# First K and Q chunks: two heads in 128 partitions and whole 128x112 TensorE transposes, with the order of all engines written anew

## The chip, the cores and the metric

The kernel runs on one core of one Trainium2 chip. The metric is device time in microseconds (us), from the first to the last instruction and what lies around them. Matrix products run on TensorE (PE; PEld is its weight load), elementwise work on VectorE (DVE), ScalarE (ACT) and GpSimd (POOL), and SyncE (SP) issues most of the DMAs.

## The reference

A recurrent attention (delta rule) over 4 batches x 8 heads, 768 steps, head size 48, and a feed-forward layer on its result:

```python
k_n = k / (np.linalg.norm(k, axis=-1, keepdims=True) + 1e-06)
for t in range(S):                       # per batch and head, state is 48x48
    y[t] = q[t] @ state
    v_old = state.T @ k_n[t]
    state = state + beta[t] * outer(k_n[t], v[t] - v_old)
x = y as [3072 tokens, 384]
h = x @ w_in                             # [3072, 2048], weights are float64
g = h * tanh(log(1 + exp(h)))            # mish
out = (g @ w_out).astype(float32)        # [3072, 384]
```

The weights reach the chip as float64 bit patterns (12.6 MB in all) and are turned on it into a high and a low single-precision part.

## The kernel before, in words

**Tiling.** The 768 steps are cut into 12 chunks of 64 steps. The 32 (batch, head) pairs stand as 16 pairs of heads; one head of a pair uses partitions 0 to 63, the other 64 to 127, and `h` 0 or 1 names the first or second 8 pairs. For a chunk the kernel forms `kt`, the keys with head size in partitions (48 rows at 0 or at 64), the products `pg` of keys with keys, a triangular solve of them on DVE in small column steps (`early`, tiles `pr` and `gt`), merges on PE (`ma`, `mb`), then the products `ta`, `tb`, `gq`, `pz`, and at the end `py`, `ps` (output and new state of the chunk). The first two chunks are solved together by `early(0)`.

**Feed-forward.** The chunk's output is transposed (`xt`) and goes through `g1` (tile `h`, 18 products of 128x256 for each of 8 pieces of the layer) and `g2` (tile `acc`, 12 products of 128x384 each), on all 12 chunks. PE does this in the gaps of the attention of later chunks.

**Weights.** There are 28 weight tiles, `ri` (512 KB each, of `w_in`) and `ro` (384 KB each, of `w_out`). `convert` clamps the upper words on DVE (L1328), scales them on ACT (L1331), shifts and joins the words on DVE (L1341, L1345), rounds on ACT (L1349) and forms the low part on PE, ACT or by an adding DMA (L1357, L1361, L1366, L1368). The first `mish` on ACT waits until 21 tiles have passed L1331.

**Start.** `loads` issues the DMAs in the order of the list `d0` (here `"k0","k1","b","a","q",2,"v",...`, a number being so many weight tiles). The keys of chunk 0 are loaded straight into `xx`, where the state update of the chunk wants them (`load_k`), those of chunk 1 and the queries of chunk 0 into plain tiles `kn1`, `qn0` (`load_plain`), each with 64 partitions for one head of the pair. `turn_k` and `turn_q0` turn them with `turned`, one product with a 64x64 identity for each head: 16 for each half of a chunk. Ahead of a key turn a product with zeros (L1405) fills the whole PSUM tile, since the turned rows leave gaps. `keep_warm` puts products with zeros (`warm`, L1868, 107 in all) on PE where it would stand still.

**What sets the order.** Every engine's order is fixed by the program. The table `TT` gives each step a rank, and the program is issued in that rank; an engine does its own instructions in that order and waits where one is not ready. `SLOT` gives each tile a buffer. The program gives its DMAs eight counters in turn: a DMA is issued once the one that had its counter before it has landed.

Of the kernel before, what the change touches and what calls it, by code (L numbers as in the profile page):

```python
# [10 lines left out]
F32 = mybir.dt.float32  # L11
# [9 lines left out]
F64_MOST = 122879.9921875  # L21
LOW = 'pppppppppddddddddddddddddddd'
# [7 lines left out]
def bcast_in(ap, n):  # L30
# [5 lines left out]
    'loadk0': [0],  # L36
    'warm0.501': [1],
    'warm30.601': [2],
    'loadk1': [3],
    'loadi1': [4],  # L40
    'turn_k(0,0)': [5],
    'loadq': [6],
    'turn_k(0,1)': [7],
    'loado13': [8],
    'turn_k(0,0).0>1': [9],
    'early0': [10, 20, 23, 24, 31, 41, 43, 48, 52, 54, 55, 56, 57, 61, 62, 64, 67, 74, 77, 79, 85, 86, 93, 104, 106, 107, 111, 113, 117, 121, 122, 131, 140, 141, 142, 507, 922],
    'turn_k(1,0)': [11],
    'loada': [12],
    'loadb': [13],
    'unit(1,)': [14],  # L50
    'early0.0>1': [15],
    'turn_k(0,1).0>1': [16],
    'turn_k(1,0).0>1': [17],
    'turn_k(1,1)': [18],
    'loadi0': [19],
    'turn_k(1,1).0>1': [21],
    'early0.1>1': [22],
    'loado2': [25],
    'loadi2': [26],
    'early0.2>1': [27],  # L60
    'warm46.601': [28],
    'warm11.802': [29],
    'early0.3>1': [30],
    'warm12.1': [32],
    'loado1': [33],
    'cv1': [34, 63, 73, 76, 95, 139, 145, 177, 1062],
    'turn_beta()': [35],
    'turn_q0(0,)': [36],
    'cv0': [37, 45, 58, 70, 78, 144, 149, 173, 728],
# [12 lines left out]
    'loadi3': [60],
    'warm11.503': [65],
    'cv25': [66, 123, 200, 289, 509, 510, 514, 520, 529],
    'warm11.502': [68],
    'cv5': [69, 112, 164, 189, 190, 198, 201, 230, 1378],
    'warm12.2': [71],
    'loadi4': [72],
    'warm11.9': [75],
    'warm29.5': [81],  # L90
    'warm0.601': [82],
    'loado0': [83],
    'cv11': [84, 96, 234, 249, 264, 275, 281, 308, 478],
# [2022 lines left out]
```

## Time and profile before

| | us |
|---|---|
| median of 3 runs | 654.91 (654.89 to 658.72) |
| the profiled execution | 655.69 |
| its span, first to last instruction | 653.8 |
| PE busy | 629.3 (96%) |
| DVE busy | 383.2 (59%) |
| ACT busy | 288.4 (44%) |
| POOL busy | 78.5 (12%) |

The busy shares are means over stages with different limits, so the profile is read by stage: the lead (up to about 83 us, where the first chunk's `py` starts), the stretch in which the feed-forward starts while weights are still converted (to about 165 us), and the rest. A row of the trace gives the start and length in us, the engine, the line, the output and input tiles, the number of instructions merged, and in brackets the idle time before and what ended it. The profile counts a single-precision product with an identity of 64 as two instructions.

### The profile page before, as it was taken

The page shows a single profiled execution, that of the slowest core. Times are in us where ns is not written, and L with a number is a line of the kernel's source. Part 1 is how long each engine was busy: PE and PEld are TensorE (multiplying, and loading weights), DVE is VectorE, ACT ScalarE, POOL GpSimd, SP SyncE. Part 2 cuts the span into 40 slices and gives each one's busy share as a digit, 9 for nine tenths or more (in the row PEclk, how much of TensorE's full clock was granted, in tenths as well). Part 3 has the DMA queues.
Part 4 walks back from the last instruction along what each step waited for, and adds up shares of the span by engine and source line. Part 5 has one row for each costly group of instructions (what it writes and reads, how often), then busy time and mean ns, then how long its engine had stood idle before and what let it go on. Part 6 is the DMA issues. An engine that isn't in the chain of part 4 may idle for free.

```text
span 653.8 us, 22428 instructions
## 1 busy us (share of the span) xinstructions
PE 629.3 (96%) x9881; PEld 584.3 (89%) x9890; DVE 383.2 (59%) x834; ACT 288.4 (44%) x556; POOL 78.5 (12%) x117
## 2 busy tenths in 40 slices
PE   8899899998999999999999999999999999999997
PEld 6664679998989988999899999999989999999996
DVE  1376679999597998674866737667543322412120
ACT  2233688844464344433542445433434534333241
POOL 5011022234100130020200010210011100000000
PEclk9999799999999999999999999999999999999999
DMA  9996056963312333223123231312301312001011
GB/s 237 322 266 119 4 89 99 164 110 74 58 23 45 70 50 50 53 34 58 36 45 55 46 55 26 57 20 38 61 2 32 70 27 49 2 2 25 1 24 25
DMA packets 155600, 42.84 MB, mean 66 GB/s; under 512 B 146384, under 2 KB 150992, under 8 KB 155504
## 3 DMA queue, kind: packets, MB, share of 16 engines
q1 hardware_dynamic: 150608, 36.73, 28.0%
q0 software_dynamic: 2736, 4.20, 3.8%
q8 instruction: 78, 1.28, 0.8%
q10 hardware_dynamic: 2160, 0.49, 0.4%
q14 instruction: 18, 0.15, 0.1%
HBM read 32.47 MB, written 4.72 MB: 57 GB/s over the span
## 4 chain that ended last, share of the span: by engine, by line
PE 70%; DVE 12%; SPq 6%; DMA 4%; ACT 3%; issue 3%; POOL 0%; DVEq 0%; POOLq 0%
PE acc L1843 23%; PE h L1809 22%; SPq L1271 6%; PE gq L1650 4%; PE warm L1868 3%; PE py L1650 3%; PE pg L1464 2%; PE kp L1398 2%; PE pz L1650 2%; DVE g L1826 2%; DVE pr L1522 2%; PE ps L1650 2%; DVE gt L1524 2%; PE tb L1650 1%; PE ta L1650 1%
## 5 line engine op out<-in xcount | busy, mean ns | idle before, releaser
L1809 PE MATMUL h<-x,wi 128*128 128x256 f32 x1728 | 221.8, 284 | 2.6 <-ACT e L1824 2.6
L1843 PE MATMUL acc<-wo,g 128*128 128x384 f32 x1152 | 218.7, 341 | 0.1
L1809 PEld LDWEIGHTS h<-x,wi 128*128 128x128 f32 x1728 | 212.9, 188 | 6.6 <-ACT e L1824 3.2
L1843 PEld LDWEIGHTS acc<-wo,g 128*128 128x128 f32 x1152 | 198.9, 188 | 2.0 <-DVE g L1826 0.5
L1826 DVE TENSOR_TENSOR g<-e,g 128x512 fp32r<-128x512 f32 x96 | 67.1, 703 | 118.6 <-ACT g L1825 118.3
L1824 ACT ACTIVATE e<-h 128x512 f32<-128x512 f32 x96 | 57.3, 598 | 79.8 <-PE h L1809 61.6
L1825 ACT CAST g<-e 128x512 fp32r<-128x512 f32 x96 | 59.0, 620 | 71.3 <-PE acc L1843 70.5
L1522 DVE TENSOR_TENSOR pr<-gt 128x58 f32<-128x58 f32 (+9 forms) x164 | 60.3, 368 | 3.9
L1524 DVE TENSOR_TENSOR gt<-gt,pr 128x58 f32<-128x58 f32 (+9 forms) x164 | 58.1, 355 | 3.9
L1628 POOL TENSOR_TENSOR vt<-vt,ne 128x384 f32<-128x384 f32 x24 | 22.3, 941 | 203.4 <-DMA vt<-in_v_dram 123.6
L1635 DVE STREAM_TRANSPOSE xx<-xx 128x1024 f32<-128x1024 f32 x20 | 24.8, 1241 | 32.1 <-DMA xx<-in_q_dram 27.8
L1650 PE MATMUL gq<-xx,kt 48*64 48x112 f32 (+1 forms) x768 | 42.1, 256 | 1.2 <-issue 1.0
L1707 DVE TENSOR_TENSOR xx<-gq,amask 64x256 f32<-64x256 f32 x96 | 40.2, 419 | 4.8 <-PE gq L1650 4.1
L1650 PEld LDWEIGHTS py<-xx 128*64 128x64 f32 x768 | 37.8, 138 | 4.1 <-issue 1.8
L1650 PE MATMUL py<-xx 128*64 128x48 f32 x768 | 41.2, 224 | 0.1
L1650 PEld LDWEIGHTS pz<-vt,tt 64*64 64x64 f32 x768 | 33.8, 138 | 7.3 <-issue 4.4
L1650 PEld LDWEIGHTS gq<-xx,kt 48*64 48x64 f32 x768 | 37.0, 133 | 2.4 <-issue 2.2
L1650 PE MATMUL pz<-vt,tt 64*64 64x48 f32 x768 | 37.5, 234 | 1.2 <-issue 1.2
L1650 PE MATMUL ps<-xx 128*48 128x48 f32 x704 | 37.6, 208 | 0.0
L1729 ACT COPY xx<-pz 64x384 f32<-64x384 f32 x48 | 22.8, 475 | 26.4 <-PE gq L1650 20.1
L1704 DVE TENSOR_TENSOR vt<-vt,gq 128x192 f32<-128x192 f32 x44 | 15.4, 351 | 32.2 <-PE gq L1650 31.6
L1557 POOL COPY tt<-d 32x512 f32<-32x512 f32 x40 | 27.6, 690 | 39.7 <-PE pz L1650 21.0
(128 smaller groups left out, 612.3 us busy)
## 6 DMA issues: line engine op xcount, KB each, us to landing
ri<-in_moe_w_in_dram SPq DMA_DIRECT2D x12, 512.0 KB, 7.5
ro<-in_moe_w_out_dram SPq DMA_DIRECT2D x16, 384.0 KB, 7.2
kt<-in_k_dram SPq DMA_DIRECT2D x76, 64.0 KB, 2.9
vt<-in_v_dram SPq DMA_DIRECT2D x48, 96.0 KB, 3.1
out_dram<-o SPq DMA_DIRECT2D x48, 96.0 KB, 2.2
xx<-in_k_dram SPq DMA_DIRECT2D x46, 96.0 KB, 2.9
xx<-in_q_dram SPq DMA_DIRECT2D x80, 32.0 KB, 2.3
wo<-mo POOLq DMA_DIRECT2D x9, 192.0 KB, 3.5
```

The source lines that it names most:

```text
L1271: m = (nc.scalar if turns[0] else nc.sync).dma_start(out=dst, in_=src)
L1522: nc.vector.tensor_tensor(out=pv, in0=nj, in1=xj, op=ALU.mult)
L1524: nc.vector.tensor_tensor(out=below, in0=below, in1=pv, op=ALU.add)
L1557: nc.gpsimd.tensor_copy(out=tt2[r, t2, :, c0:c0 + 32], in_=dts[g][r, t2])
L1635: nc.vector.transpose(x, x)
L1650: last[:] = [nc.tensor.matmul(*a, start=True, stop=True)]
L1707: nc.vector.tensor_tensor(out=x[r, p4, hh, D:D + C], in0=ps[r, :, d:], in1=bcast_mid(amask[r], 4), op=ALU.mult)
L1809: nc.tensor.matmul(h[:, f2, :], wt["i", f * P // WI * NCH + c][:, i2, f0:f0 + P], x[:, c, :], start=(i == 0), stop=(i == 3 * NCH - 1))
L1824: for d, f in ((0.7, lambda: nc.scalar.activation(e, h, AF.Mish)), (0.7, lambda: nc.scalar.copy(out=gg[:, 0], in_=e)), (0.8, lambda: nc.ve ...
L1825: (0.7, lambda: nc.scalar.copy(out=gg[:, 0], in_=e)),
L1826: (0.8, lambda: nc.vector.tensor_tensor(out=gg[:, 1], in0=e, in1=gg[:, 0], op=ALU.subtract))):
L1843: nc.tensor.matmul(acc[t], gg[:, a, f2, ts_], wt["o", f][:, i2, :], start=(f == 0 and i == 0), stop=(f == NF - 1 and i == 2))
```

## The change: what it does

`load_plain` now loads the keys of chunks 0 and 1 and the queries of chunk 0 into a tile of 128 partitions x 8 x 112: partitions 0 to 63 hold 64 steps of one pair of heads, 64 to 127 those of the next pair, and the 112 columns hold both heads of the pair, 48 columns each, with a gap of 16 that DVE sets to zero. `turned` is four TensorE transposes of 128x112 for each half of a chunk, where there were 16 products; the product with zeros is gone. Since the keys of chunk 0 no longer come through `xx`, a new step `"x"` of `d0` loads them there later, from the same place in memory. The copies out of PSUM take 112 partitions instead of 128. `ON_POOL = (0, 0)` leaves both shifts and clamps of `convert` on DVE. The tables `TT` and `SLOT` are written anew, so every engine's order differs in places.

```diff
+ON_POOL = (0, 0)
...
 TT = {
-    'loadk0': [0],
-    'warm0.501': [1],
-    'warm30.601': [2],
-    'loadk1': [3],
+    'warm0.501': [0],
+    'loadk0': [1],
+    'warm11.601': [2],
+    'loadi0': [3],
...
-              dw=51.0, nw=0, d0=["k0","k1","b","a","q",2,"v",3,4,"s",3,"p",5,"k2",4,7,"k3"], un=(21.0, 21.1), tb=8.8,
+              dw=51.0, nw=0, d0=["k0","k1","b","a","q",2,"v",3,"x",4,"s",3,"p",5,"k2",4,7,"k3"], un=(21.0, 21.1), tb=8.8,
...
+    WN = D + C
 
     def load_plain(key, src, both=False):
-        t = nat[key] = placed(mp, "g", 3, [P, NP, D], F32, key)
-        for hh in range(2):
-            turns[0] = both and hh == 1
-            load(t[64 * hh:64 * hh + 64], src[hh])
+        pool, tag, nb = (ap, "kt", 4) if key == "qn0" else (mp, "g", 3)
+        t = nat[key] = placed(pool, tag, nb, [P, PB, WN], F32, key)
+        nc.vector.memset(t[:, :, D:C], 0.0)
+        for pp in range(2):
+            turns[0] = both and pp == 1
+            for hh in range(2):
+                c0 = C - C * hh
+                load(t[C * pp:C * pp + C, :, c0:c0 + D], src[hh].rearrange("t (a b) d -> b t a d", b=2)[pp])
         turns[0] = False
 
-    def turned(ps, h, hh, src):
-        r, r0 = slice(64 * hh, 64 * hh + 64), 64 - 64 * hh
-        for p in range(PB):
-            nc.tensor.matmul(ps[r0:r0 + D, p, :], src[r, p], ident[r, r], start=True, stop=True)
+    def turned(ps, h, src):
+        for a in range(4):
+            nc.tensor.transpose(ps[:WN, 2 * a:2 * a + 2, :].rearrange("p a b -> p (a b)"), src[:, 4 * h + a], ident)
 
     def turn_k(n, h):
...
-        nc.tensor.matmul(ps.rearrange("p a b -> p (a b)"), zb[:, 0:P], zb[:, :512], start=True, stop=True)
-        for hh in range(2):
-            turned(ps, h, hh, nat["kn1"][:, PB * h:PB * h + PB] if n else xx[h][:, :, hh, D + C:])
+        turned(ps, h, nat[f"kn{n}"])
 
         def out():
-            nc.scalar.copy(out=kts[n][:, PB * h:PB * h + PB].rearrange("p a b c -> p a (b c)"), in_=ps)
+            nc.scalar.copy(out=kts[n][:WN, PB * h:PB * h + PB].rearrange("p a b c -> p a (b c)"), in_=ps[:WN])
...
     def turn_q0(h):
...
-        for hh in range(2):
-            turned(ps, h, hh, nat["qn0"][:, PB * h:PB * h + PB])
+        turned(ps, h, nat["qn0"])
...
+        elif x == "x":
+            for h in range(2):
+                load_k(0, h)
+            give("x0")
...
-            if m == 0:
-                for h in range(2):
-                    load_k(0, h, both=True)
-                give("x0")
-            elif m == 1:
-                load_plain("kn1", kk[:, C:2 * C], both=True)
+            if m < 2:
+                load_plain(f"kn{m}", kk[:, C * m:C * m + C], both=True)
```

**PE, the first instructions after the opening `warm` products.** `kp` is the PSUM tile of a turn, `kn` a plain tile of keys. Before:

```order
L1405 MATMUL kp_0_125<-zero 128x512
L1398 MATMUL kp_0_125<-ident,xx_100 48x64 x16
...
L1405 MATMUL kp_1_146<-zero 128x512
L1398 MATMUL kp_1_146<-ident,xx_101 48x64 x16
L1464 MATMUL pg_0_169<-kt_124 32x64 x32
...
L1405 MATMUL kp_0_203<-zero 128x512
L1398 MATMUL kp_0_203<-ident,kn_119 48x64 x16
```

Now:

```order
L1403 MATMUL kp_0_136<-ident,kn_113 112x128 x4
L1403 MATMUL kp_1_141<-ident,kn_113 112x128 x4
L1869 LDWEIGHTS zero
L1869 MATMUL warm<-zero 128x512
...
L1466 MATMUL pg_0_154<-kt_135 32x64 x32
L1466 MATMUL pg_1_191<-kt_135 32x64 x32
L1403 MATMUL kp_0_231<-ident,kn_125 112x128 x4
```

Each turn is four instructions instead of 17, and both halves of chunk 0 have their `pg` before chunk 1 is turned. Before the first turn there are eight `warm` products now, and there were four.

**DVE, from the start to the first transpose of the solve.** `d` takes the masked `pg`; `ri` are weight tiles. Before:

```order
L1254 COPY xx_101<-ident 64x8x48 x2
L1468 TENSOR_TENSOR d_167<-pg_0_169,lmask 128x256
L1468 TENSOR_TENSOR d_167<-pg_1_250,lmask 128x256
L1468 TENSOR_TENSOR d_167<-pg_0_287,lmask 128x256
L1468 TENSOR_TENSOR d_167<-pg_1_320,lmask 128x256
L1476 STREAM_TRANSPOSE gt_364<-d_167 128x1024
```

Now:

```order
L1329 TENSOR_SCALAR ri_121<-ri_121 128x512
L1393 MEMSET kn_125 128x8x16
L1393 MEMSET qn_224 128x8x16
L1342 TENSOR_SCALAR ri_121<-ri_121 128x512
L1346 SCALAR_TENSOR_TENSOR mi_243<-ri_121 128x512
L1329 TENSOR_SCALAR ri_146<-ri_146 128x512
L1470 TENSOR_TENSOR d_152<-pg_0_154,lmask 128x256
L1470 TENSOR_TENSOR d_152<-pg_0_249,lmask 128x256
L1470 TENSOR_TENSOR d_152<-pg_1_191,lmask 128x256
L1329 TENSOR_SCALAR ri_187<-ri_187 128x512
L1470 TENSOR_TENSOR d_152<-pg_1_286,lmask 128x256
L1478 STREAM_TRANSPOSE gt_340<-d_152 128x1024
```

Three clamps of weight tiles stand ahead of the last `d`, and the one of `ri_121` stands ahead of the memset of `kn_125`, the tile that the keys of chunk 1 are turned from.

**SP, where the weights' loads end.** `kt` is the load of chunk 2's keys here, `q` that of chunk 1's queries, `xx_100` and `xx_101` those of keys for the state update. Before:

```order
L1271 DMA ri_918<-in_moe_w_in_dram 128x1024
L1271 DMA ro_938<-in_moe_w_out_dram 128x768
L1271 DMA q_991<-in_q_dram 32x16x32 x8
L1271 DMA ri_1124<-in_moe_w_in_dram 128x1024
L1271 DMA ro_1127<-in_moe_w_out_dram 128x768
L1271 DMA kt_1143<-in_k_dram 32x16x32 x8
L1271 DMA xx_100<-in_k_dram 64x8x48 x2
L1271 DMA xx_101<-in_k_dram 64x8x48 x2
```

Now:

```order
L1272 DMA ro_946<-in_moe_w_out_dram 128x768
L1272 DMA xx_100<-in_k_dram 64x8x48 x2
L1272 DMA xx_101<-in_k_dram 64x8x48 x2
L1272 DMA q_1020<-in_q_dram 32x16x32 x8
L1272 DMA ro_1037<-in_moe_w_out_dram 128x768
L1272 DMA ro_1041<-in_moe_w_out_dram 128x768
L1272 DMA ro_1044<-in_moe_w_out_dram 128x768
L1272 DMA xx_100<-in_k_dram 64x8x48 x2
L1272 DMA kt_1202<-in_k_dram 32x16x32 x8
```

The first two `xx` rows are the new step `"x"`. The load of chunk 2's keys, which stood ahead of the `xx` load of chunk 1 (which waits for `ps` of chunk 0), now stands behind it.

## Rows read from the trace of the kernel before

**Rows 1.** The page's part 4, the chain that ended last, by engine and line.

```profile
PE 70%; DVE 12%; SPq 6%; DMA 4%; ACT 3%; issue 3%; POOL 0%; DVEq 0%; POOLq 0%
```

**Rows 2.** Stages: length, busy us (instructions) of each engine, PE clock, DMA share, GB/s.

```profile
28.00:54.00 26.00, 25.50 (x183) 14.73 (x185) 21.54 (x61) 8.22 (x18) 2.06 (x3) 1.00 0.91 257
54.00:83.00 29.00, 25.09 (x711) 16.80 (x713) 17.36 (x44) 16.33 (x37) 3.14 (x4) 0.88 0.23 51
83.00:165.00 82.00, 78.41 (x1480) 72.88 (x1484) 75.47 (x169) 59.96 (x117) 25.70 (x32) 1.00 0.63 107
165.00:654.00 489.00, 476.55 (x7122) 459.83 (x7120) 265.66 (x556) 198.01 (x376) 39.26 (x57) 1.00 0.22 38
```

**Rows 3.** PE in order of time: start, length in us, line, tiles, count, idle before.

```profile
1.54 1.89 PE L1868 MATMUL warm<-zero 128*128 128x512 bf16 x4 [1.54 <-DVE zero L1224]
...
4.23 3.22 PE L1398 MATMUL kp<-ident,xx 64*48 64x64 f32 x32 [0.38 <-DMA xx<-in_k_dram]
7.39 0.61 PE L1405 MATMUL kp<-zero 128*128 128x512 bf16 x1
...
11.11 1.93 PE L1464 MATMUL pg<-kt 48*32 48x64 f32 x64
...
26.24 1.43 PE L1464 MATMUL pg<-kt 48*32 48x64 f32 x42 [1.55 <-issue]
...
29.85 1.52 PE L1906 MATMUL beta<-spare,eye 16*32 16x192 f32 x16
31.30 5.88 PE L1398 MATMUL qp<-ident,qn 64*48 64x64 f32 x64
37.52 8.21 PE L1868 MATMUL warm<-zero 128*128 128x512 bf16 x34 [0.33 <-issue]
```

**Rows 4.** PE, the transposes that the kernel already does, same columns.

```profile
88.31 0.82 PE L1781 MATMUL xt<-ident,yy 128*128 128x128 f32 x6
```

**Rows 5.** DVE in order of time, the first solve and chunk 2's keys, same columns.

```profile
27.71 0.42 DVE L1468 TENSOR_TENSOR d<-pg,lmask 128x256 f32<-128x256 f32 x1 [3.16 <-PE pg L1464]
28.16 1.92 DVE L1476 STREAM_TRANSPOSE gt<-d 128x1024 f32<-128x1024 f32 x1
...
46.92 0.86 DVE L1707 TENSOR_TENSOR xx<-gq,amask 64x256 f32<-64x256 f32 x2 [3.29 <-PE gq L1650]
...
52.18 1.91 DVE L1534 STREAM_TRANSPOSE tt<-gt 128x1024 f32<-128x1024 f32 x1
...
99.30 1.24 DVE L1433 STREAM_TRANSPOSE kt<-kt 128x1024 f32<-128x1024 f32 x1
```

**Rows 6.** ACT in order of time: the first copy of turned keys, same columns.

```profile
7.49 0.59 ACT L1410 COPY kt<-kp 128x512 f32<-128x512 f32 x1 [3.27 <-PE kp L1398]
```

**Rows 7.** SP's queue in order of time, issue of DMAs, same columns.

```profile
0.82 1.67 SPq L1271 DMA_DIRECT2D xx<-in_k_dram  x2
...
42.30 9.99 SPq L1271 DMA_DIRECT2D q<-in_q_dram  x8
...
53.34 7.31 SPq L1271 DMA_DIRECT2D kt<-in_k_dram  x8
84.81 3.72 SPq L1271 DMA_DIRECT2D xx<-in_k_dram  x4
88.62 5.15 SPq L1271 DMA_DIRECT2D kt<-in_k_dram  x8
```

**Rows 8.** DMA issues from 0 to 60 us: count, KB each, median us to landing.

```profile
ri<-in_moe_w_in_dram SPq DMA_DIRECT2D x12, 512.0 KB, 7.5
...
xx<-in_k_dram SPq DMA_DIRECT2D x2, 96.0 KB, 3.7
```

**Rows 9.** Stretches of 1 us with the granted clock, columns as in rows 2.

```profile
71.00:72.00 1.00, 0.00 (x0) 0.00 (x0) 0.95 (x3) 0.95 (x3) 0.00 (x0) 1.00 0.00 0
...
74.00:75.00 1.00, 1.00 (x34) 0.94 (x32) 0.41 (x2) 0.27 (x1) 0.00 (x0) 0.50 0.00 0
```

**Rows 10.** The chain of waits where chunk 0's output starts: start, length, what.

```profile
82.98 0.25 PE py L1650 x4
```

More of the change, by code (lines that the diff above doesn't have):

```diff
@@ L51 @@
[L51 to L69, printed above, removed]
@@ new lines @@
+    'g2.0.2': [465],
+    'turn(1,).0>1': [466],
+    'g1.0.4.0>1': [467],
+    'g1.0.4.0>2': [471],
+    'g1.0.5.0>1': [473],
+    'g1.0.4.0>3': [474],
+    'turn(1,).0>2': [490],
+    'g1.0.5.0>2': [492],
+    'g1.0.5.0>3': [495],
+    'prep(2,)': [508],
+    'g2.0.3': [511],
+    'turn(1,).0>3': [513],
+    'g2.0.4': [515],
+    'turn(1,).0>4': [516],
+    'g2.0.5': [527],
+    'g1.0.6': [528],
+    'g1.0.6.0>1': [533],
+    'g1.0.6.0>2': [536],
+    'g1.0.6.0>3': [538],
+    'g1.0.7': [539],
@@ new lines @@
+    'g1.3.7': [912],
+    'g1.3.7.0>1': [913],
+    'g1.3.6': [915],
+    'early4.2>1': [916],
+    'g2.3.1': [919],
+    'turn(4,)': [920],
+    'g1.3.5.0>2': [922],
+    'turn(4,).0>3': [924],
+    'g1.3.4': [927],
+    'scale_v(5,1)': [928],
+    'ats_z[4,1]+s_gq[5,0].0>3': [929],
+    'g2.3.2': [930],
+    'turn_q(5,1)': [932],
+    'g1.3.5.0>3': [934],
+    'early4.3>1': [935],
+    'g1.3.4.0>1': [936],
+    'ats_b[5]+s_a[6]': [937],
+    'turn(4,).0>1': [938],
+    'ats_b[5]+s_a[6].0>1': [939],
@@ new lines @@
+    'g1.3.4.0>2': [940],
+    'g2.3.3': [942],
+    'turn(4,).0>2': [943],
+    'g1.3.4.0>3': [944],
+    'turn(4,).0>4': [945],
+    'ats_b[5]+s_a[6].0>2': [946],
+    'ats_z[5,0]+s_gq[5,1]': [947],
+    'g1.4.1': [948],
+    'prep(6,)': [949],
+    'g2.3.4': [950],
+    'g1.3.7.0>2': [951],
+    'ats_z[5,0]+s_gq[5,1].0>1': [952],
+    'g1.3.7.0>3': [953],
+    'ats_z[5,0]+s_gq[5,1].0>2': [954],
+    'g1.3.6.0>1': [955],
+    'g2.3.5': [956],
+    'g1.4.1.0>1': [958],
+    'g1.3.6.0>2': [960],
@@ new lines @@
+    'g1.4.2.0>1': [989],
+    'g1.4.2.0>2': [991],
+    'g1.4.6': [992],
+    'g1.4.0.0>2': [993],
+    'ats_y[5,1]': [994],
+    'g1.4.0.0>3': [998],
+    'g2.3.7.0>2': [999],
+    'ats_z[5,1]+s_gq[6,0].0>3': [1000],
+    'g2.4.0': [1004],
+    'g1.4.6.0>1': [1007],
+    'ats_y[5,1].0>1': [1008],
+    'g2.4.1': [1009],
+    'g1.4.3': [1010],
+    'g1.4.6.0>2': [1011],
+    'g1.4.5': [1012],
+    'g1.4.2.0>3': [1013],
+    'g1.4.3.0>1': [1014],
+    'turn(5,)': [1015],
+    'g1.4.6.0>3': [1016],
@@ new lines @@
+    'g1.5.4': [1141],
+    'g1.5.5.0>1': [1142],
+    'ats_y[6,1].0>1': [1145],
+    'g1.5.3.0>3': [1146],
+    'ats_b[7]+s_a[8]': [1147],
+    'g1.5.4.0>1': [1148],
+    'turn_q(7,1)': [1149],
+    'ats_b[7]+s_a[8].0>2': [1150],
+    'g2.5.3': [1151],
+    'turn(6,)': [1152],
+    'g1.5.4.0>2': [1153],
+    'g1.5.4.0>3': [1154],
+    'ats_b[7]+s_a[8].0>1': [1155],
+    'turn(6,).0>3': [1156],
+    'g1.5.7': [1157],
+    'turn(6,).0>4': [1158],
+    'g2.5.4': [1159],
+    'turn(6,).0>1': [1160],
@@ new lines @@
+    'g1.7.2.0>1': [1329],
+    'g2.6.7.0>2': [1330],
+    'g1.7.2.0>2': [1331],
+    'g1.7.3': [1333],
+    'ats_y[8,1].0>1': [1334],
+    'g1.7.2.0>3': [1335],
+    'g2.7.0': [1336],
+    'g1.7.3.0>1': [1337],
+    'turn(8,)': [1339],
+    'g1.7.3.0>2': [1341],
+    'g1.7.3.0>3': [1344],
+    'g1.7.4.0>1': [1345],
+    'g2.7.1': [1346],
+    'g2.7.2': [1347],
+    'turn_q(9,1)': [1349],
+    'g1.7.7.0>2': [1350],
+    'turn(8,).0>3': [1351],
+    'g1.7.7.0>3': [1353],
+    'g1.7.4.0>2': [1355],
@@ new lines @@
+    'g1.9.6.0>1': [1506],
+    'g2.9.3': [1507],
+    'g1.9.6.0>2': [1508],
+    'g1.9.5.0>1': [1509],
+    'g2.9.4': [1510],
+    'g1.9.5.0>2': [1511],
+    'turn(10,).0>1': [1512],
+    'ats_z[11,1]+s_gq[12,0]': [1513],
+    'g1.9.7': [1514],
+    'g1.9.5.0>3': [1515],
+    'turn(10,).0>2': [1516],
+    'ats_z[11,1]+s_gq[12,0].0>1': [1517],
+    'g1.10.1': [1518],
+    'ats_y[11,1]': [1519],
+    'g1.9.7.0>1': [1520],
+    'ats_y[11,0]': [1521],
+    'g2.9.5': [1522],
+    'g1.9.6.0>3': [1523],
@@ new lines @@
+    'g2.9.7.0>2': [1543],
+    'turn(11,).0>2': [1544],
+    'g1.10.2.0>1': [1545],
+    'g2.10.0': [1546],
+    'g1.10.2.0>2': [1547],
+    'g2.10.1': [1548],
+    'g1.10.3.0>2': [1549],
+    'g1.10.6': [1550],
+    'g1.10.3.0>3': [1551],
+    'turn(11,).0>3': [1552],
+    'g1.10.5': [1553],
+    'g1.10.2.0>3': [1554],
+    'g1.10.6.0>1': [1555],
+    'g1.10.4': [1556],
+    'turn(11,).0>4': [1557],
+    'g2.10.2': [1558],
+    'g1.10.6.0>2': [1559],
+    'g1.10.4.0>1': [1560],
+    'g1.11.0': [1561],
@@ L1027 @@
+    'g2.11.7.0>2': [1620],
 }
 SLOT = {
[72 rows of a table removed]
[72 rows of a table added]
 }
@@ L1860, in moe @@
         return g1, g2
+    zb = zero.bitcast(BF16)
     warm = placed(ph, "h", 2, [P, 512], F32, "warm")
```

926 lines of the change are left out of this document (807 added, 119 removed), and 963 rows, old and new, of tables (SLOT, TT).

## The prediction

> **What bounds the kernel now.** I read the chain of waits first, then the busy times by stage, then the lead engine by engine in order of time. The chain that ends last is 70% PE [rows 1]. By stage [rows 2], PE is busy 476.6 of the 489 us from 165 us on and 78.4 of the 82 us before that, so from about 83 us to the end the kernel is a queue of PE work, with DVE nearly full beside it up to 165 us (75.5 of 82). Whatever lets that queue begin earlier is returned at the end almost whole. So the question is what sets the start of chunk 0's `py`, at 82.98 us [rows 10].
>
> In the lead PE looks busy as well (25.5 of 26 us from 28 to 54), but there the reader must look at what it does: 34 `warm` products take 8.21 us [rows 3], and they only fill. What is waited for is the solve on DVE. It starts with the transpose at 28.16, right after the last `d` at 27.71, which had waited 3.16 us for PE [rows 5]. PE had been late with `pg` because of the turns: a half turn takes 3.22 us, with 0.61 for the zeros ahead of it, and four of these stand among the `pg` [rows 3]. DMA is not what was late there: the first turn started at 4.23, and the later ones ran back to back.
>
> **The change, part by part.** *The turns.* Removed are four half turns of keys at 3.25 us, four products with zeros at about 0.55 (7.39 to the next product at 7.93), and 5.88 us for the queries [rows 3]: 13.0 + 2.2 + 5.9 = 21.1 us of PE. Added are 24 transposes (three tiles of 8). The nearest row is that of the kernel's own 128x128 transposes, six in 0.82 us, 0.14 each [rows 4], so 3.3 us. PE is relieved of 17.8 us.
>
> *From the start to the last `d`.* The first turn now needs four loads instead of two, two on each queue. The second is issued at about 1.66 (two issues in 1.67 us from 0.82 on) [rows 7] and lands 3.7 us later [rows 8]: 5.3. Eight transposes, 1.1: 6.4. The first copy out of PSUM, 0.59 [rows 6] beside the end of the transposes, lets `pg` start at about 6.8; two of them at 1.93 [rows 3] end at 10.7. Chunk 1's keys should have landed by then. Their turn 1.1, the copy 0.59 and two `pg` give 16.3, and `d`, 0.42, ends at 16.7. DVE has three clamps of weight tiles in its way now. The third tile's load waits for a counter that one of the chunk 1 key loads holds, so I put its issue near 9 and its landing, 7.5 later [rows 8], near 16.5: it just about hides beside `pg`. I take 17.1 for the last `d`, where it was 28.13: **11.0 us** earlier. The bounds: 12 if no weight holds DVE, 7 if a tile comes 4 us late. The memset of chunk 1's tile stands behind the first clamp, whose tile (issued near 2.5, landing near 10) is there before PE is free for that turn at 10.7: nothing, with 2 us to lose.
>
> *From there to the end of the solve's transposes*, 28.16 to 54.09 before. DVE stood 3.29 us for `gq` [rows 5], since PE gave it 34 `warm` products and the query turn first. Now PE ends `pg` at 16.3, and `beta` (1.52), 41 `warm` at 0.24 (8.21 / 34), and 1.1 for the query turn bring `gq` to about 29, while DVE, with over 14 us of solve behind the first transpose, comes to it after 31. The wait goes: **3.3 us**. What DVE would be late for next is its own conversions, of which fewer stand inside the solve now (nine of the tiles' rows instead of thirteen by the order); I count nothing for that. Bounds 0 and 5. The transposes end at about 39.8 instead of 54.1.
>
> *From there to `py`*, 28.9 us before. [...] Six `warm` products stand on this way instead of 14, eight at 0.24: **1.9 us**. [...]
>
> *After `py`.* The order of steps is nearly the same, and DVE has the same conversions or a few more behind it at each step. Zero, within 3 us either way for an order with other waits in 82 us where both PE and DVE are full.
>
> *Loads.* Eight more DMAs (two for chunk 1, two for the queries, four for step `"x"`) and 384 KB more. The four for `"x"` cost SP's queue 3.72 us [rows 7], behind nearly all weights, and only `py` needs them, at 66 or so: hidden. DVE has three small memsets more, under 0.5 us together.
>
> The sum: 11.0 + 3.3 + 1.9 = 16.2. The PE count gives a second view: if what stands still and what fills stays the same, the whole is shorter by the 17.8 us taken off PE. Against the profiled execution, 655.69, the sum gives 639.5. The median of the runs is 0.8 lower, so **638.7**, and I write 638.5.
>
> **The rivals.** *1. The clock falls in the start.* PE waits for the first keys from about 5 us and again before chunk 1's turn, and it no longer has 13 us of identity products. Empty time was followed by the level 0.50 at 74 us, for about 7 us [rows 2, 9]. If that comes over the four `pg`, they take twice 7.7 us, and the end moves by 4 to 8 us: 642 to 646. For it: gaps that were not there before. Against it: two `warm` products stand behind each turn of keys, and the 1.55 us that PE stood still before 26.24 [rows 3] were followed by a stage at 1.00 [rows 2]. 0.17.
>
> [...]
>
> *2. The lead shortens and what follows does not.* Chunk 2's keys now stand on SP behind a load that waits for chunk 0's `ps`. With `py` at 67, `ps` ends near 69; eight issues take 5.15 to 7.31 us [rows 7] and landing some 3: 77 to 80. DVE, which turns them at 99.30 now [rows 5], would want them at 83. The slack is 3 to 6 us. If these loads go as slowly as the eight for chunk 1's queries (9.99 [rows 7]), or weights land later than the shorter lead wants them, DVE, which is in order, holds all conversions: half the gain or more is lost, 647 to 653. 0.13.
>
> *3. Slower.* The lower clock from the first wait until the feed-forward starts. The four `warm` products at 1.54 took 0.47 each against 0.24 later [rows 3], so this price is in the rows: 69 `warm` ahead of the merges at 0.23 more are 15.9 us, `pg` 7.7 more, `beta` 1.5: 25, so 664. It decides once the filling products no longer bring the clock back, that is if level 0.50 stands in the records from 10 us to over 25 us. Against it: 41 `warm` in a row behind `beta`. 0.07.
>
> That the change doesn't do what it says is out: the order shows four transposes in place of 17 instructions at each half turn.
>
> **How the numbers follow.** Forecast 0.63, rivals 0.17, 0.13 and 0.07. The forecast's own range, from its bounds, is 630 to 646. For 8 in 10 the range goes from 628 (clock held, waits shrink) to 650, which takes in rival 1 and half of rival 2. One per cent, about what a measurement of this kernel can tell from no change, is 6.5 us: faster means below 648.4. The forecast, rival 1 and a little of rival 2 make 0.82; within, 0.11; slower, 0.07.
>
> **What would show it.** Right: the last `d` at 16 to 18 us, no wait for `gq` on DVE, the solve's last transpose near 40, `py` near 67, and from there the same distances as now. Wrong: a clock of 0.50 over `pg` or `beta` (rivals 1 and 3); DVE waiting for a `ri` load ahead of the last `d` (first term too large); DVE waiting for the DMA of `kt` between 75 and 90 us (rival 2); or a stage after `py` longer than its 82 and 489 us.

## The result, and the profile after

The changed kernel takes **635.29 us** in the median (631.34 to 640.34, four runs) against 654.9 beside it: a ratio of 0.9695, 95% interval 0.9615 to 0.9775. The forecast was 638.5, between 628 and 650. The profiled execution of the change was the longest of its four, 640.34 us with a span of 638.4. Against the 653.8 of the span before that is 15.4 us less, where my sum said 16.2. The medians are 19.6 us apart, so this execution shows less of the gain than most.

The stages of the changed kernel, columns as in [rows 2], with the two that come ahead of those:

```profile
16.00:28.00 12.00, 11.61 (x114) 5.85 (x115) 9.04 (x28) 4.63 (x12) 1.01 (x2) 0.72 0.82 243
28.00:54.00 26.00, 20.71 (x442) 11.58 (x440) 16.51 (x43) 10.38 (x22) 1.98 (x3) 0.87 0.92 284
54.00:83.00 29.00, 27.42 (x773) 20.75 (x772) 24.14 (x55) 22.96 (x48) 4.29 (x6) 0.94 0.52 106
83.00:165.00 82.00, 79.76 (x1356) 74.71 (x1353) 71.81 (x164) 54.62 (x105) 21.04 (x26) 0.98 0.63 105
165.00:638.40 473.40, 465.14 (x6822) 450.10 (x6820) 255.48 (x537) 191.00 (x363) 41.20 (x59) 1.00 0.22 38
```

The last stage is 15.4 us shorter and as full as before (465.14 of 473.40): the same queue of PE work, begun earlier. Where it was won, and where some was lost again, is in PE's lead in order of time, the view of [rows 3]:

```profile
1.53 3.59 PE L1869 MATMUL warm<-zero 128*128 128x512 bf16 x8 [1.53 <-DVE zero L1225]
...
5.82 1.93 PE L1403 MATMUL kp<-ident,kn 128*112 128x128 f32 x8 [0.69 <-DMA kn<-in_k_dram]
...
8.53 2.78 PE L1466 MATMUL pg<-kt 48*32 48x64 f32 x128
11.24 1.09 PE L1403 MATMUL kp<-ident,kn 128*112 128x128 f32 x8
...
12.69 1.13 PE L1466 MATMUL pg<-kt 48*32 48x64 f32 x65
16.39 1.35 PE L1466 MATMUL pg<-kt 48*32 48x64 f32 x63 [2.56 <-issue]
17.67 1.52 PE L1907 MATMUL beta<-spare,eye 16*32 16x192 f32 x16
...
24.93 1.04 PE L1403 MATMUL qp<-ident,qn 128*112 128x128 f32 x8
...
42.11 0.68 PE L1589 MATMUL mb<-tt,ym 32*32 32x16 f32 x59
47.16 0.29 PE L1589 MATMUL mb<-tt,ym 32*32 32x16 f32 x5 [4.38 <-issue]
```

The three turns are 1.93, 1.09 and 1.04 us, where four half turns of 3.25 and a query turn of 5.88 stood. Longer than any such stop before (1.55 us, [rows 3]) are two marked "issue", with no engine and no transfer named: 2.56 us in the middle of `pg`, and 4.38 five products ahead of the end of the first `mb`. On DVE, the view of [rows 5], the solve begins at 18.24; there is a short wait for `gq`, and a long one for that `mb`:

```profile
17.78 0.42 DVE L1470 TENSOR_TENSOR d<-pg,lmask 128x256 f32<-128x256 f32 x1 [2.84 <-PE pg L1466]
18.24 1.93 DVE L1478 STREAM_TRANSPOSE gt<-d 128x1024 f32<-128x1024 f32 x1
...
32.55 0.86 DVE L1707 TENSOR_TENSOR xx<-gq,amask 64x256 f32<-64x256 f32 x2 [0.67 <-PE gq L1650]
...
37.71 1.92 DVE L1536 STREAM_TRANSPOSE tt<-gt 128x1024 f32<-128x1024 f32 x1
47.51 0.29 DVE L1592 TENSOR_TENSOR tt<-tt,mb 128x128 f32<-128x128 f32 x1 [6.42 <-PE mb L1589]
...
143.26 1.91 DVE L1543 STREAM_TRANSPOSE d<-gt 128x1024 f32<-128x1024 f32 x1
```

The last row closes the second solve (157.08 before). `py` begins at 69.03 (82.98 before, [rows 10]).

### The profile page after: what moved, and what is told of

The parts are those of the page before. It is cut to its first block, busy times and chain, and to the rows that moved or that the text cites. A ratio compares the mean times of both kernels' runs of the same rounds, so it can differ in the third digit from the quotient of the medians.

```text
span 638.4 us, 22132 instructions
## 1 busy us (share of the span) xinstructions
PE 616.2 (97%) x9718; PEld 570.5 (89%) x9718; DVE 382.0 (60%) x837; ACT 288.1 (45%) x555; POOL 77.8 (12%) x117
## 3 DMA queue, kind: packets, MB, share of 16 engines
q8 instruction: 77, 1.26, 0.8%
## 4 chain that ended last, share of the span: by engine, by line
PE 74%; DVE 12%; SPq 4%; issue 4%; DMA 4%; POOL 1%; ACT 0%; DVEq 0%; POOLq 0%
PE acc L1843 26%; PE h L1809 25%; PE gq L1650 4%; SPq L1272 4%; PE warm L1869 3%; PE py L1650 3%; PE pg L1466 2%; PE pz L1650 2%; PE ps L1650 2%; DVE pr L1524 2%; DVE gt L1526 2%; PE tb L1650 1%; PE ta L1650 1%; DVE xx L1707 1%; DMA kt<-in_k_dram 1%
## 5 line engine op out<-in xcount | busy, mean ns | idle before, releaser
L1843 PEld LDWEIGHTS acc<-wo,g 128*128 128x128 f32 x1152 | 202.1, 190 | 2.1 <-issue 0.3
L1524 DVE TENSOR_TENSOR pr<-gt 128x58 f32<-128x58 f32 (+9 forms) x164 | 58.1, 354 | 4.0
L1526 DVE TENSOR_TENSOR gt<-gt,pr 128x58 f32<-128x58 f32 (+9 forms) x164 | 56.3, 343 | 4.1
L1869 PE MATMUL warm<-zero 128*128 128x512 bf16 x107 | 29.9, 434 | 1.5 <-DVE zero L1225 1.5
```

The source lines that it names most:

```text
L1524: nc.vector.tensor_tensor(out=pv, in0=nj, in1=xj, op=ALU.mult)
L1526: nc.vector.tensor_tensor(out=below, in0=below, in1=pv, op=ALU.add)
L1843: nc.tensor.matmul(acc[t], gg[:, a, f2, ts_], wt["o", f][:, i2, :], start=(f == 0 and i == 0), stop=(f == NF - 1 and i == 2))
L1869: nc.tensor.matmul(warm, zb[:, 0:P], zb[:, :512], start=True, stop=True)
```

## The experiments

All are edits of the changed kernel, but for e11, an edit of the kernel before. Ratios are to the kernel before on the same chip. Two landmarks go with them, `py`'s start and that row of the second solve (us, from the one profiled execution of each, so good to some 3 us: the changed kernel and e0 are the same program, and their `py` is 3.0 us apart).

| kernel | median us | ratio (95%) | last `d` begins | `py` | second solve |
|---|---|---|---|---|---|
| before | 654.9 | 1 | 27.71 | 82.98 | 157.08 |
| changed | 635.29 | 0.9695 (0.9615 to 0.9775) | 17.78 | 69.03 | 143.26 |
| e0, the same again | 634.77 | 0.9672 (0.9627 to 0.9718) | 17.86 | 66.05 | 140.52 |
| e1, old turns | 650.93 | 0.9942 (0.9898 to 0.9987) | 23.63 | 72.54 | 152.99 |
| e2, old order | 645.36 | 0.9851 (0.981 to 0.9892) | 17.49 | 69.75 | 144.70 |
| e10, old query turn | 638.91 | 0.9726 (0.9689 to 0.9762) | 15.83 | 68.30 | 142.18 |
| e11, before with 4 more `warm` | 654.75 | 0.997 (0.9941 to 0.9999) | 21.10 | 80.41 | 156.19 |
| e3, 32 pairs ahead | 645.94 | 0.985 (0.98 to 0.9899) | 15.95 | 68.49 | 145.22 |
| e6, 64 pairs ahead | 646.98 | 0.9838 (0.9779 to 0.9896) | 17.36 | 68.55 | 144.30 |
| e5, 96 pairs ahead | 635.58 | 0.967 (0.9629 to 0.971) | 15.72 | 66.05 | 141.80 |
| e4, 127 pairs ahead | 638.62 | 0.9712 (0.9666 to 0.9758) | 16.16 | 68.19 | 141.78 |
| e7, three buffers | 635.8 | 0.9679 (0.9631 to 0.9728) | 15.57 | 63.35 | 138.73 |
| e8, small fillers | 634.59 | 0.9682 (0.9627 to 0.9738) | 15.65 | 65.69 | 139.06 |
| e9, e5 and e7 | 639.87 | 0.9747 (0.9694 to 0.9801) | 17.28 | 69.28 | 147.81 |

**e0.** No edit.

> The changed kernel once more, beside the experiments on the same chip. Both theories: the same ratio to the kernel before as in its first runs, 0.965 to 0.977 (632 to 640 us). Its single runs lay between 631 and 640; if PE's standing still for 'issue' and the low clock after it differ from run to run, they will again spread by several us, where the kernel before spreads by less.

The same time, and the two long stops at the same two products (63 left of `pg`, 5 left of `mb`), 2.24 and 4.65 us. So the stops belong to the program and not to one execution. The end of the solve's transposes is nearly that of the changed kernel's trace too (39.24 for 39.63):

```profile
37.33 1.91 DVE L1536 STREAM_TRANSPOSE tt<-gt 128x1024 f32<-128x1024 f32 x1
```

**e1: the order and step `"x"` of the change, the turns of before.**

```diff
...
-            nc.tensor.transpose(ps[:WN, 2 * a:2 * a + 2, :]..., src[:, 4 * h + a], ident)
...
+                nc.tensor.matmul(ps[r0:r0 + D, p, :], src[r, PB * h + p], ident[r, r], start=True, stop=True)
...
```

> The new order and the new step x, but the turns as before: heads of a pair in partitions 0-63 and 64-127, 16 products with a 64x64 identity for each half turn and the product with zeros ahead of it. Theory T (the gain is PE's time in the turns, which brings the solve forward): PE has 17.8 us more, the last d goes from 18 to 28-30 us, and the time to 648-656 us. Rival O (the gain comes from the order written anew): 633-642 us.

The order alone gives 0.6%; with the transposes it is 3.3%. So in this order the transposes are worth some 16 us (650.93 less 634.77). In the profiles (648.5 and 634.6 us) only part of that is there when `py` starts: 5.8 us at the last `d`, 6.5 at `py`, 12.5 at the second solve, 13.9 at the end. Behind `py` both programs do the same work, so more than half of the 13.9 us appears where no turn stands, and these runs do not show why.

**e2: the change with the old order** (the table of times and the slots of before, the new step `"x"` put at its old place).

```diff
-    'warm0.501': [0],
-    'loadk0': [1],
+    'loadk0': [0],
+    'loadx': [213.5],
...
```

> The transposes of the change, but the order of all engines and the buffers of the kernel before (the new load step x stands just ahead of the load of chunk 1's queries). Theory T: the last d comes at 17-20 us and most of the gain is there, 636-645 us. Rival O: 648-655 us, since the old order keeps its waits.

1.5%: in the old order the transposes bring the last `d` as early (17.49), and give about 10 us. Against the kernel before this is the plainest case of the prediction's mechanism: 10.2 us at the last `d`, 13.2 at `py`, 12.4 at the second solve and, by span, 11.6 at the end. The two parts together give more than the 10 and 4.6 us of each alone. How much of the remaining 6 is a real joint effect I leave open, since e3 shows differences as large that come from neither.

**e10: only the query turned by the old products**, with 71 small ones added behind `gq`, for the reason that e3 gives.

```diff
...
-        turned(ps, h, nat["qn0"])
...
+                nc.tensor.matmul(ps[r0:r0 + D, p, :], src[r, PB * h + p], ident[r, r], start=True, stop=True)
...
+                for _ in range(71):
+                    nc.tensor.matmul(warm[:, :16], zb[:, 0:P], zb[:, :16], start=True, stop=True)
```

> The keys are turned as in the changed kernel, the queries by the old products (64 pairs on TensorE for 8), and 71 small products stand ahead of the 28 warm products behind gq, so that from there on the code blocks end where they ended (56 + 71 = 127). Theory T (what TensorE gives up ahead of gq comes back at the end, the prediction's second step): the query turn takes 6 to 8 us instead of 1.0, DVE waits 5 to 7 us for gq instead of 0.67, the solve's last transpose comes 4.5 to 6.5 us later than 37.7, and the time is 638 to 641.5 us against 634.8 of e0. Rival D (the keys' turns carry all of the gain, and what the queries' turn takes is slack before later waits): DVE waits for gq all the same, but the time is 633 to 637 us.

The turn took 3.23 us and not 6 to 8: the 5.88 of [rows 3], from which I had it, was at the slower pace (e11, below). It is 2.2 us more than the 1.04 of the transposes, and DVE's wait grew by the same, from 0.67 to 2.93:

```profile
23.07 3.23 PE L1431 MATMUL qp<-ident,qn 64*48 64x64 f32 x64
```

```profile
33.00 0.86 DVE L1716 TENSOR_TENSOR xx<-gq,amask 64x256 f32<-64x256 f32 x2 [2.93 <-PE gq L1659]
```

The time is within the range of theory T, some 4 us over e0; the two intervals overlap, so the wait is shown, its price only about.

**e11: the kernel before, with eight `warm` at the start where it has four.** This came from a thing that I had misread. In [rows 3] a `warm` product takes 0.47 us at 1.54 and 0.24 on average from 37.52 on, though the clock's column in [rows 2] reads 1.00 over 28 to 54 us.

```diff
...
+        more = 0 if begun else 4
+        begun.append(1)
-        for _ in range(n):
+        for _ in range(n + more):
```

> The kernel before, with eight warm products at the very start where it has four. In its trace everything on TensorE up to 38 us goes at the pace of the lower speed (a half turn 3.22 us, warm 0.47, pg 1.93, beta 1.52), although the clock's column reads 1.00 there; in e1, with the same products behind eight warm ones, half turns took 1.96 and 1.80. Theory S (part of the gain is that TensorE comes up to speed early, and not that the transposes are few): with eight warm products the first half turns take 1.8 to 2.0 us, the last d ends at 20 to 25 us instead of 28.13, and the time is 644 to 652 us against the kernel before's 655. Rival T (only the number of products counts): half turns stay at 3.2 us or the end does not move, 653 to 658 us.

PE's lead in e11, then DVE's:

```profile
1.54 3.59 PE L1872 MATMUL warm<-zero 128*128 128x512 bf16 x8 [1.54 <-DVE zero L1224]
...
5.28 1.80 PE L1398 MATMUL kp<-ident,xx 64*48 64x64 f32 x32
...
9.07 1.10 PE L1464 MATMUL pg<-kt 48*32 48x64 f32 x64
...
19.55 1.50 PE L1464 MATMUL pg<-kt 48*32 48x64 f32 x46 [3.04 <-issue]
...
24.68 5.88 PE L1398 MATMUL qp<-ident,qn 64*48 64x64 f32 x64
```

```profile
21.10 0.42 DVE L1468 TENSOR_TENSOR d<-pg,lmask 128x256 f32<-128x256 f32 x1 [4.41 <-PE pg L1464]
...
40.29 0.86 DVE L1707 TENSOR_TENSOR xx<-gq,amask 64x256 f32<-64x256 f32 x2 [3.26 <-PE gq L1650]
45.54 1.91 DVE L1534 STREAM_TRANSPOSE tt<-gt 128x1024 f32<-128x1024 f32 x1
```

A half turn takes 1.80 us in place of 3.22, the same instructions; behind the stop that ends at 19.55 the pace is the slow one again (`qp` 5.88, as before). There the column agrees with it. These are the stretches of the query turn, in the kernel before and then in e11, columns as in [rows 2]:

```profile
31.30:37.18 5.88, 5.88 (x68) 5.74 (x66) 5.44 (x18) 3.51 (x7) 2.06 (x3) 1.00 0.84 164
24.68:30.56 5.88, 5.88 (x68) 5.74 (x66) 5.46 (x18) 3.53 (x7) 2.06 (x3) 0.50 1.02 403
```

The same work takes the same 5.88 us, once under a column of 1.00 and once of 0.50. So in the kernel before PE had run the whole lead to about 38 us at the slower of the two paces measured (a `warm` product in 0.47 us, not 0.24), under a column of 1.00. On the mechanism theory S was right: the last `d` is 6.6 us earlier, and so is the end of the solve's transposes (47.45 for 54.09). On the time it was wrong: 1.4 us. At `py` 2.6 of the 6.6 were left, at the second solve 0.9. In between PE is on the chain, with its own fillers and conversions, at the lower speed again over part of it (granted clock 0.71 from 54 to 83 us, 0.88 in [rows 2]). **Here an earlier `d` alone did not come back at the end.** Whether it was PE's queue behind it, as long as before, that took it, or the longer time at the lower speed, this run does not separate.

**e3: 32 small products ahead of the first `warm`.** This asks what "issue" is. Theory C: PE's code has not arrived. The profile's page has one row of instruction packets that fits PE by its count:

```profile
q8 instruction: 77, 1.26, 0.8%
```

77 packets of 16.4 KB. Counted along PE's stream, the products ahead of the stops in the changed kernel are 221, 602, 729, 856 and 983: steps of 127, or three times 127. That is one packet to 127 pairs of weight load and product (9718 pairs / 77 = 126).

```diff
...
+            for _ in range(32):
+                nc.tensor.matmul(warm[:, :16], zb[:, 0:P], zb[:, :16], start=True, stop=True)
```

> The changed kernel with 32 small products with zeros (16 columns, 64 instructions) ahead of the first warm product. Theory C (PE's idle time that ends with 'issue' is instruction code that arrives late, in blocks of a fixed number of instructions): the stop in chunk 1's pg, after 65 of 128 pairs now, comes after about 33 pairs, and the one in chunk 0's mb, after 59 of 64, after about 27. Rival D (the stop belongs to the place, a buffer or a copy that is late): it stays after 65 and 59. Time: theory C -4 to +4 us, as the stops fall elsewhere; rival D +1 us for the products.

The stops moved by 32 products to the row: 95 left of `pg` where 63 were, 37 of `mb` where 5 were.

```profile
14.24 1.54 PE L1466 MATMUL pg<-kt 48*32 48x64 f32 x95 [2.31 <-issue]
...
43.78 0.72 PE L1589 MATMUL mb<-tt,ym 32*32 32x16 f32 x37 [4.56 <-issue]
```

So the stops stand at fixed counts of PE's stream (221 and 602 products ahead of them, as without the 32) and not at a place of the program. That it is code which arrives late is theory C's reading of these counts; nothing else in the traces goes by them. The kernel before has stops at the same steps: the 1.55 us of [rows 3] stand behind 349 products in its trace (221 and a packet are 348), and the empty microsecond of [rows 9] (70.91 to 72.43 us) ends behind 1109 (221 and seven packets are 1110; the trace lacks some records, as it holds 99 of the 107 `warm`). The time was a miss: 11 us more than e0, though `d` was earlier.

**e4, e5, e6: 127, 96 and 64 pairs ahead** in place of 7, 5 and 3 of the first `warm`, so that nothing starts later; in e4 the stream is longer by one whole packet. The count in the edit is 134, 101 and 67.

```diff
...
+            for _ in range(134):
+                nc.tensor.matmul(warm[:, :16], zb[:, 0:P], zb[:, :16], start=True, stop=True)
```

> 134 small products with zeros (16 columns) take the place of the first 7 warm products, so TensorE's instruction stream is longer by 127 pairs of weight load and product. Theory C (TensorE stops where its code has not arrived, once every 127 pairs): the stops come back to the places that they have in the changed kernel, one in the second pg behind 65 products and one of about 4.5 us in the first mb behind 59, and the time is 632 to 641 us (the changed kernel ran in 634.8 beside e0). Rival X (e3 was slow because products were added ahead, wherever the code falls): 645 us or more.

> 101 small products with zeros take the place of the first 5 warm products: the stream is longer by 96 pairs. Theory C: the stop that stood behind 59 products of the first mb falls about 32 pairs further on from there (96 is 31 short of a block), behind the first mb, where TensorE waits for DVE anyway; no stop above 2.5 us between 40 and 60 us, and 628 to 638 us. Rival X (anything added ahead costs): 645 us or more.

> 67 small products with zeros take the place of the first 3 warm products: the stream is longer by 64 pairs. Theory C: the block's end that stood behind 59 products of the first mb now falls at that mb's beginning, and its code is fetched beside warm products: no stop above 2.5 us between 40 and 60 us, but one of 2 to 4 us at the second pg's beginning; 630 to 640 us. Rival X: 645 us or more.

With a whole packet the stops are back at their places (in the trace 62 and 4 products are left, one fewer than with none added), and so is the time, nearly:

```profile
14.82 1.29 PE L1466 MATMUL pg<-kt 48*32 48x64 f32 x62 [1.52 <-issue]
...
45.95 0.29 PE L1589 MATMUL mb<-tt,ym 32*32 32x16 f32 x4 [4.72 <-issue]
```

96 pairs, three times what e3 adds, cost nothing, while 32 and 64 cost some 11 us each by their ratios. It is therefore not the added work. What is left is the place of the stops, but that is argued and not shown, since the stops themselves do not add up to 11 us. My forecasts by place were poor, though: e5's stop left the merge as said, only to stand as long behind the second one, and e6's time is outside its range with stops of 2.60 us at most. That one stood ahead of `beta`: ACT's copy of it came late, and DVE waited 3.12 us inside the solve where it waits 0.56 in e0, and e6 is 2.5 us behind e0 at `py`.

```profile
48.21 0.39 PE L1578 MATMUL ma<-tu,d 16*32 16x16 f32 x11 [5.54 <-issue]
```

**e7: a third buffer for `mo`.** No instruction changes. Behind `py` the chain of the changed kernel's trace (start, length, what) goes through DVE and these transfers:

```profile
79.16 2.35 DMA kt<-in_k_dram
...
89.12 4.13 DMA wo<-mo
...
95.79 3.46 DMA kt<-in_k_dram
...
121.25 4.95 DMA wi<-mi
```

```diff
...
-        a = spare[:, :n] if third else placed(mp, "w", 2, [P, 512], F32, f"m{kind}{i}")[:, :n]
+        a = spare[:, :n] if third else placed(mp, "w", 2, [P, 384 if SLOT[f"m{kind}{i}"] == 2 else 512], F32, f"m{kind}{i}")[:, :n]
```

In the table of slots six `mo` go to slot 2, and the others take turns on 0 and 1.

> Every instruction as in the changed kernel; only the buffers mo and mi, which VectorE writes and the GpSimd queue's transfers read, are three instead of two, the third for mo alone. Theory W (between 83 and 145 us the end of the second solve on VectorE is set by its waits of 4 to 5 us for transfers that free these buffers): these waits go, the second solve ends 4 to 8 us earlier, and the time is 627 to 631 us. Rival: the waits only stand in front of others (chunk keys landing, TensorE's stops), and the time is 633 to 637 us, as of the changed kernel.

No gain, the same ratio as e0 (0.9679 and 0.9672): theory W is out as the limit of the time. Its profiled execution has an early second solve (138.73), but the median is that of e0.

**e8: the 69 `warm` between `beta` and the merges with 16 columns.**

```diff
...
+            w = 16 if 12 < len(warmed) <= 81 else 512
-            nc.tensor.matmul(warm, zb[:, 0:P], zb[:, :512], start=True, stop=True)
+            nc.tensor.matmul(warm[:, :w], zb[:, 0:P], zb[:, :w], start=True, stop=True)
```

> The 69 warm products between beta and the first merge are made with 16 columns in place of 512: as many instructions and the same ends of code blocks, but about 2 us of work instead of 17.7. Theory K (the fillers are needed, since without them TensorE falls to its lower clock in the lead, rival 3 of the prediction): the granted clock reads 0.50 over most of 20 to 54 us, the merges' products take twice as long, and the time is 640 to 652 us. Rival D (up to the merges VectorE's solve sets the time, and TensorE only has to be there): gq comes earlier, VectorE's 0.67 us of waiting goes, the solve's last transpose stays at 37 to 38 us, and the time is 632 to 639 us.

The clock did fall and stay down for nearly 30 us, in stretches of 4 us:

```profile
18.00:22.00 4.00, 0.11 (x2) 0.14 (x4) 3.13 (x14) 3.37 (x8) 0.16 (x1) 0.53 0.99 323
...
26.00:30.00 4.00, 0.00 (x0) 0.00 (x0) 3.69 (x17) 1.64 (x3) 0.00 (x0) 0.50 0.83 289
...
42.00:46.00 4.00, 1.23 (x8) 0.83 (x9) 0.89 (x4) 0.99 (x2) 0.00 (x0) 0.50 1.02 407
46.00:50.00 4.00, 3.64 (x121) 1.96 (x120) 2.00 (x5) 1.78 (x5) 0.46 (x1) 0.63 1.04 230
```

and the time is that of e0 (the solve's last transpose began at 35.07, not at 37 to 38, since the stop in `pg` was 1.25 us here). Theory K is out, rival D holds: up to the merges DVE's solve sets the pace, PE only has to be there. (With the fillers cut PE had that much less to do; fillers of full size at the lower clock were not run.)

**e9: e5 and e7 together.**

```diff
...
+            for _ in range(101):
+                nc.tensor.matmul(warm[:, :16], zb[:, 0:P], zb[:, :16], start=True, stop=True)
...
-        a = spare[:, :n] if third else placed(mp, "w", 2, [P, 512], F32, f"m{kind}{i}")[:, :n]
+        a = spare[:, :n] if third else placed(mp, "w", 2, [P, 384 if SLOT[f"m{kind}{i}"] == 2 else 512], F32, f"m{kind}{i}")[:, :n]
```

> The 96 pairs of e5 and the third buffer of e7 in one kernel. If each takes a wait that stands by itself (the stop in the merges, the wait for a free buffer behind the second solve), the time is 629 to 633 us, under the changed kernel's 634.8 of e0; if both only move a wait to another place, as their own times of 635.6 and 635.8 say, it is 633 to 638 us.

Outside both ranges, and by the medians slower than either part (the intervals overlap a little); in its profile the merges have stops of 2.40 and 2.76 us, and the second solve comes at 147.81, later than in any other version with the transposes. No version here beats the changed kernel by more than its own spread (629.86 to 640.34 in ten runs).

## Why the prediction was right

Point by point, from the profiled executions: before against the change, and against e0, the same program in another execution:

| step of the prediction | said, us | measured, us | in e0, us |
|---|---|---|---|
| start to the last `d` | -11.0 | -9.9 (ends 18.20 for 28.13) | -9.8 (18.28) |
| to the end of the solve's transposes | -3.3 | -4.5 (39.63 for 54.09) | -5.0 (39.24) |
| to `py` | -1.9 | +0.5 (69.03 for 82.98) | -2.1 (66.05) |
| after `py` | 0 | -1.4 (569.4 to the end for 570.8) | -2.3 (568.5) |
| sum | -16.2 | -15.4 | -19.2 |

The mechanism is the one forecast: nearly all of the gain is there when `py` starts. That the sum comes within 1 us of the first execution is in part luck, as its errors have both signs. The medians, 19.6 us apart, lie nearer to e0.

*The last `d`.* Right in size, by errors that cancel. The first eight transposes took 1.93 us and not 1.1, and the stop of 2.56 us marked "issue" stood in the last `pg`. Against that `pg` goes at 0.017 us a product behind the second turn (1.13 / 65), where the 1.93 for 64 of [rows 3] is 0.030. The stop is a term that I did not have; the cause of the other two is the reading that e11 corrected. The column's 1.00 was no proof of full speed, and the 21.1 us of removed work were a price at the lower speed: at the higher one a half turn is 1.80 and the query turn 3.23 (e10). PE's busy time fell by 13.1 us in the change (629.3 to 616.2) and by 16.8 in e0, where my second view had 17.8. No weight held `d` on DVE, as said, and the three new memsets took 0.17 us each.

*The wait for `gq`.* It shrank from 3.29 to 0.67 us, nearly the 3.3 that I took; e10 gives 2.2 us of it back by making the query's turn 2.2 us longer. The step gave more than that, though. Here are its stretches before and now, from the solve's first transpose to its last:

```profile
28.16:54.09 25.93, 25.44 (x184) 14.64 (x185) 21.50 (x60) 8.22 (x18) 2.06 (x3) 1.00 0.91 255
18.24:39.63 21.39, 21.39 (x124) 10.07 (x117) 19.11 (x55) 8.48 (x19) 1.01 (x2) 0.87 0.82 247
```

DVE is busy for 2.4 us less (21.50 to 19.11): these are the conversions that no longer stand inside the solve, which I saw and put at nothing.

*The way to `py`.* The weakest step. The fillers went, as said (six are left), but DVE stood 6.42 us for an `mb` that stood itself, 4.38 us under "issue". I had no term for such stops, though the 1.55 us of "issue" in [rows 3] and the empty microsecond of [rows 9] were such stops: from 0 to 83 us PE has 6.7 us under "issue" in the kernel before (none above 1.6), 9.4 in the changed one and 7.9 in e0. In e0 the step came out as forecast all the same (-2.1), with DVE 6.70 us at that `mb`; its later stops are shorter (0.30 and 0.74 us for 0.91 and 1.33), and its clock is 1.00 from 54 to 83 us for 0.94. So the mechanism of this step was incomplete, and its number is good to about 3 us. That the faster lead makes these stops longer is my reading, which no run separates. The bounds that I set to this step in the range of 630 to 646, 8 us gained and 3 lost, were an estimate of mine that no run shows; the two executions lost 0.5 and gained 2.1.

*Behind `py`* the distances are those of before, as said: 74.2 us to the second solve (74.1), 495.1 from there (496.7).

*Rival 1* happened, without its price. PE stood from 13.8 to 16.39, and the granted clock fell, in stretches of 2 us:

```profile
14.00:16.00 2.00, 0.00 (x0) 0.00 (x0) 0.95 (x3) 0.00 (x0) 0.00 (x0) 1.00 1.03 301
16.00:18.00 2.00, 1.61 (x68) 1.34 (x72) 0.22 (x1) 0.00 (x0) 0.00 (x0) 0.77 0.96 300
18.00:20.00 2.00, 2.00 (x19) 0.74 (x12) 1.97 (x2) 0.71 (x3) 0.00 (x0) 0.50 1.01 315
...
24.00:26.00 2.00, 2.00 (x14) 1.39 (x13) 1.86 (x7) 0.38 (x1) 0.53 (x1) 1.00 0.92 329
```

But `pg` was nearly past (its last 63 products took 1.35 us, where 1.13 went for the 65 ahead of the stop), and `beta` and fillers bore it. The prices that I gave it and rival 3 for `pg` and `beta` were wrong in any case: the rows that I doubled ran at the lower speed already (a product of `pg` in 0.030 us, 0.017 now). Why the first turn was slow is open: behind eight `warm` the ordinary products of e11 ran at the faster pace from 5.28 on (1.80 us a half turn), while in the changed kernel the transposes from 5.82 on took 1.93 us, and 1.09 in the next turn. PE had stood 0.69 us ahead of them, but in e6 the same turn took 1.05 us after 1.26 us of standing. *Rival 2* happened in part: `kt` is on the chain twice, 2.35 and 3.46 us, in this execution, not in e0's. *Rival 3* did not happen: the clock was back at 1.00 from 24 to 26 us, after some 6 us of fillers. Of its price e8 shows that the lower clock from 18 to 46 us costs nothing when the fillers are small (634.59 us for 634.77 in e0); my 25 us added up TensorE's time where TensorE was not the limit, but with fillers of full size that was not run.

**What stays open.** Why e3 and e6 lose 11 us and e5 none. In the profiles e3 is 2.4 us behind e0 at `py`, 4.7 at the second solve and 7.9 at the end (642.5 for 634.6); the chain of e3 runs there through the transfers `wo`, `kt`, `wo` and `wi` (5.04, 5.15, 5.58 and 4.96 us), where e0's has one of that length (5.04, `wi`). DVE itself stood only 1.6 us for `wo` from 66 to 165 us, and 0.4 in e0. A third buffer alone gains nothing, so I can name these transfers but not call them the cause. By the same token the 10 us of e2 and the 4.6 of e1 hold only to within what such a shift of PE's stream may be worth, up to 11 us here, and some of the 20 us of the change may be a good place. So that the transposes bring `d` and `py` forward is shown; how the 20 us divide between them, the order and the place of the stops is not. e11 says the same from the other side: its 6.6 us went between the solve and the end in three parts (4.1, 1.7 and, by span, the rest), with no single wait that I could show.

## What to carry to other kernels

Take the durations of an engine's work from rows of the same pace, and test the pace with one instruction of known length (here `warm`: 0.24 or 0.47 us), not with the clock's column. Time won early on the chain need not arrive at the end: a `d` 6.6 us earlier gave 1.4 us where PE's work was left as long (e11), and one 5.8 us earlier went with 16 us where PE was busy for 15 us less (627.8 in e1, 612.5 in e0). Take a landmark from more than one execution before explaining a step of 2 us by it. After an edit that changes how many instructions an engine has, count where its stops fall before reading a difference of one per cent as the edit's own.

## What the runs showed of the hardware that I had not expected

- PE's stops under "issue" in the changed kernel stand 127 pairs of weight load and product apart, or three times 127 (behind 221, 602, 729, 856 and 983). Such stops last up to 5.54 us (e5); the two longest of the changed kernel, 4.38 and 2.56 us, fall in stretches with a DMA share near 1 (0.99 from 44 to 46 us, 1.03 from 14 to 16), and the 128 products of the first `pg` last 2.78 us. The page's 77 instruction packets of 16.4 KB make 126 pairs each; that PE waits for them there is a reading. One stop of 1.5 us stands where the DMA engines were idle ([rows 9], share 0.00). The stop moves with the count of products and not with the work: 32 added, 32 products earlier; 127 added, the same place.
- Small products at the start that do nothing can cost 1.8% of this kernel's time or none, and not by their number: 0.985 with 32, 0.984 with 64, 0.967 with 96, 0.971 with 127. They shift where the stops fall; that this is the cause is not shown.
- The clock's column reads 1.00 from the start of the trace of before although PE runs at the slower pace: four `warm` in 1.89 us at 1.54, 0.47 each for 0.24 later, and that pace up to about 38 us (the query turn 5.88 us under 1.00, as in e11 under 0.50). With eight `warm` at the start in place of four the same half turns went from 3.22 to 1.80 us.
- A granted clock of 0.50 to 0.53 from 18 to 46 us cost nothing with the fillers cut to 16 columns (e8, 634.59 us for 634.77 in e0): DVE was busy for 18.2 of the 20 us from 18 to 38, PE for 7.3.
